# Layer scale with residual (x + gamma·y) on one core: row blocks of 4, 64 and 60 in place of 8, 60 and 60, and stores released by VectorE

## The chip, the core and the metric

The kernel runs on one core of a Trainium2 chip. The metric is the device time of one execution in microseconds (us); lower is better. Before the change it is 119.94 us, the median of three runs (119.84 to 120.05). The profiled execution spans 118.5 us from its first to its last instruction; the time counts a little more than that span.

## What is computed

```python
x: [1024, 16, 512] bf16      y: [1024, 16, 512] bf16      gamma: [512] bf16
out = x + gamma * y          # gamma is broadcast over the last dimension
```

Flattened, x, y and the output are 16,384 rows of 512 bf16 values, 1,024 bytes a row. Each of the 128 SBUF partitions holds 128 rows, so "60 rows" below always means 60 rows in each of 128 partitions: 60 KiB a partition and 7,680 KiB in all. The kernel reads 33.55 MB and writes 16.78 MB. The only arithmetic is one multiplication and one addition per element.

## The kernel before

All loads are issued by SyncE into one DMA queue, all stores by ScalarE into another. The 128 rows of a partition are cut into three blocks, and each block is one contiguous run of device memory per partition. VectorE works on four pieces: the pieces of 15 and 45 rows together are the second block.

```python
BLOCKS = [8, 60, 60]
PIECES = [8, 15, 45, 60]
SP = [                       # what SyncE loads, in this order: (tensor, first row, end row, slot in x_sb)
    ('y', 0, 8),
    ('y', 8, 68),
    ('x', 8, 68, 0),
    ('y', 68, 128),
    ('x', 68, 128, 15),      # its slots 15 to 75 overlap the slots 0 to 60 of x's rows 8 to 68
    ('x', 0, 8, 0),
]
ACT = [('g',), ('s', 8, 68), ('s', 68, 128), ('s', 0, 8)]     # gamma's load, then the three stores
EARLY = (2, 0)               # the first two loads stand ahead of the start barrier
RELEASE = ('x', 68, 128, 15)
DVE = [('m', 0), ('m', 1), ('m', 2), ('a', 2), ('a', 1), ('m', 3), ('a', 3), ('a', 0)]
```

y has its own 128 KiB a partition and is multiplied and added to in place; the stores read y_sb. x has a smaller buffer of 75 rows, so a later load of x waits until the sums that read its slots are done: x's rows 68 to 128 wait for the sum of piece 2 (`a, 2`), x's rows 0 to 8 for the sum of piece 1 (`a, 1`).

The stores have a gate of their own besides the sums that they need. TensorE waits for the load of x's rows 68 to 128, and then releases ScalarE (`s_go`) and VectorE (`s_rel`):

```python
    _take(s_load[RELEASE], 16, nc.tensor)      # TensorE waits for x's rows 68..128
    nc.tensor.sem_inc(s_go, 1)                 # ScalarE may issue the first store
    nc.tensor.sem_inc(s_rel, 1)                # VectorE may add piece 3
# ... (cut)
    for kind, *args in DVE:
        c = args[0]
        yt = y_sb[:, starts[c] : starts[c + 1], :]
        if kind == "m":
            need(y_loads, c)
            g = gamma_sb[:, None, :].to_broadcast([P, PIECES[c], D])
            nc.vector.tensor_tensor(out=yt, in0=yt, in1=g, op=MULT).then_inc(s_dve, 1)
            open_mults += 1
        else:
            need(x_loads, c)
            # ... (cut: waits for VectorE's own products)
            nc.vector.tensor_tensor(out=yt, in0=xt, in1=yt, op=ADD).then_inc(s_add, 1)
```

The gate keeps the stores out of the way of the large loads. gamma is spread over the 128 partitions by one small matmul with a row of ones, and copied from PSUM to SBUF.

Of the kernel before, what the change touches and what calls it, by code (L numbers as in the profile page):

```python
# [3 lines left out]

BLOCKS = [8, 60, 60]

PIECES = [8, 15, 45, 60]


SP = [
    ('y', 0, 8),
    ('y', 8, 68),
    ('x', 8, 68, 0),
    ('y', 68, 128),
    ('x', 68, 128, 15),
    ('x', 0, 8, 0),
]
ACT = [('g',), ('s', 8, 68), ('s', 68, 128), ('s', 0, 8)]  # L20

EARLY = (2, 0)

RELEASE = ('x', 68, 128, 15)

DVE = [('m', 0), ('m', 1), ('m', 2), ('a', 2), ('a', 1), ('m', 3), ('a', 3), ('a', 0)]
MULT, ADD = mybir.AluOpType.mult, mybir.AluOpType.add


def _take(sem, n, eng):  # L30


    return eng.wait_ge(sem, n).then_inc(sem, -n)  # L33


def kernel(
# [9 lines left out]
    nc = tc.nc  # L46
# [8 lines left out]
    rows = N // P  # L55
    n = len(PIECES)
    assert sum(PIECES) == rows
    starts = [sum(PIECES[:c]) for c in range(n + 1)]
    dt = xf.dtype
    edges = [sum(BLOCKS[:c]) for c in range(len(BLOCKS) + 1)]  # L60
    assert edges[-1] == rows

    def rows_of(t, a, b):

        c = max(c for c in range(len(BLOCKS)) if edges[c] <= a)
        assert b <= edges[c + 1]
# [6 lines left out]
    y_sb = nc.alloc_sbuf_tensor("y_sb", [P, rows, D], dt).ap()  # L73
    x_loads = [w for w in SP + ACT if w[0] == "x"]
    y_loads = [w for w in SP + ACT if w[0] == "y"]
    stores = [w for w in SP + ACT if w[0] == "s"]
    for loads in (x_loads, y_loads, stores):
# [5 lines left out]
    sem = nc.alloc_semaphore  # L83
    s_gamma, s_ones, s_ps, s_dve = sem("s_gamma"), sem("s_ones"), sem("s_ps"), sem("s_dve")
    s_load = {w: sem("s_" + "_".join(map(str, w[:2]))) for w in x_loads + y_loads}
    s_add, s_go, s_rel, s_end, s_out = sem("s_add"), sem("s_go"), sem("s_rel"), sem("s_end"), sem("s_out")
    added = [a for kind, *a in DVE if kind == "a"]
    order = {a[0]: k for k, a in enumerate(added)}

    def meets(a, b, c, d):  # L90
        return a < d and c < b
# [4 lines left out]
    def x_at(row):  # L96
        return next(w[3] + row - w[1] for w in x_loads if w[1] <= row < w[2])
# [12 lines left out]
    def ring(eng, what, n_early):  # L110

        known, went = 0, False
        for k, w in enumerate(what):
            kind = w[0]
            need = frees(w) if kind == "x" else pieces_of(w[1], w[2]) + list(w[3:]) if kind == "s" else []
            need = max((order[c] + 1 for c in need), default=0)
            if kind == "s" and not went:
                _take(s_go, 1, eng)
                went = True
            if need > known:  # L120
                eng.wait_ge(s_add, need)
                known = need
            if kind == "g":
                i = eng.dma_start(out=gamma_row, in_=gamma.unsqueeze(0)).then_inc(s_gamma, 16)
            elif kind == "x":
                to = x_sb[:, w[3] : w[3] + w[2] - w[1], :]
                i = eng.dma_start(out=to, in_=rows_of(xf, w[1], w[2])).then_inc(s_load[w], 16)
            elif kind == "y":
                r = slice(w[1], w[2])
                i = eng.dma_start(out=y_sb[:, r, :], in_=rows_of(yf, w[1], w[2])).then_inc(s_load[w], 16)  # L130
            else:
                r = slice(w[1], w[2])
                i = eng.dma_start(out=rows_of(of, w[1], w[2]), in_=y_sb[:, r, :]).then_inc(s_out, 16)
            if k < n_early:
                early.append(i.ins)

    ring(nc.sync, SP, EARLY[0])
    ring(nc.scalar, ACT, EARLY[1])

# [6 lines left out]
    nc.vector.tensor_copy(out=gamma_sb, in_=gamma_ps).then_inc(s_dve, 1)  # L146
    _take(s_dve, 1, nc.vector)

    _take(s_load[RELEASE], 16, nc.tensor)
    nc.tensor.sem_inc(s_go, 1)  # L150
    nc.tensor.sem_inc(s_rel, 1)

    landed, open_mults = set(), 0

    def need(loads, c):
        for w in loads:
            if w not in landed and meets(starts[c], starts[c + 1], w[1], w[2]):
                if w == RELEASE:
                    _take(s_rel, 1, nc.vector)
                else:  # L160
                    _take(s_load[w], 16, nc.vector)
                landed.add(w)

    for kind, *args in DVE:
        c = args[0]
        yt = y_sb[:, starts[c] : starts[c + 1], :]
        if kind == "m":
# [6 lines that stand above are left out]
            if open_mults:  # L174
                _take(s_dve, open_mults, nc.vector)
                open_mults = 0
            at = x_at(starts[c])
            xt = x_sb[:, at : at + PIECES[c], :]
            nc.vector.tensor_tensor(out=yt, in0=xt, in1=yt, op=ADD).then_inc(s_add, 1)  # L179
# [44 lines left out]
```

## Time and profile before

| What | Value |
|---|---|
| time, median of 3 runs | 119.94 us (119.84 to 120.05) |
| span of the profiled execution | 118.5 us |
| VectorE busy | 70.1 us (59% of the span) |
| TensorE busy | 0.6 us |
| bytes moved by DMA | 50.33 MB, mean 425 GB/s over the span |
| a product or sum of 60 rows (128x30720) on VectorE | 16.16 us |
| of 45 rows (128x23040) | 12.16 us |
| of 15 rows (128x7680) | 4.16 us |
| of 8 rows (128x4096) | 2.29 us |

An engine's row in the profile counts its arithmetic only. The instructions that issue a DMA take about 0.4 us of their queue's time and show when a transfer was asked for, not how long it ran; the transfer's own time is from its issue to its landing. A share of DMA over a stretch is the mean over the core's 16 DMA engines. In such a stretch a packet's bytes and time are booked at one point of the packet, so short stretches swing above and below 1; stretches of several packets are to be read.

### The profile page before, as it was taken

What the parts mean: (1) busy time and instruction counts of PE and PEld (TensorE: products, weight loads), DVE (VectorE), ACT (ScalarE), POOL (GpSimd) and SP (SyncE); (2) the same over time, 40 slices, a digit from 0 to 9 for tenths busy, and PEclk for the clock granted to TensorE, in tenths of its full rate; (3) what the DMA queues carried; (4) which work ended last, traced back from release to release, by engine and by line L of the source; (5) the groups of instructions that cost most, each with busy time, mean ns of one, the idle gap of its engine ahead of it and who ended that gap; (6) DMA issues with size and microseconds to landing.
All of it is one profiled execution on the core that took longest, in us unless ns stands there. A gap on an engine that the chain in (4) does not pass through costs nothing. (4 is left out here: it accounts for less than half of the span.)

```text
span 118.5 us, 81 instructions
## 1 busy us (share of the span) xinstructions
PE 0.6 (0%) x1; PEld 0.1 (0%) x1; DVE 70.1 (59%) x10; POOL 0.2 (0%) x4
## 2 busy tenths in 40 slices
PE   0001000000000000000000000000000000000000
PEld 0000000000000000000000000000000000000000
DVE  0005400299999399999499999469999950000000
POOL 0000000000000000000000000000000000000000
DMA  5999779779779779978977977897797797797787
GB/s 180 506 602 394 332 332 663 332 332 663 332 332 663 332 332 601 394 332 352 643 332 332 663 332 332 384 633 332 332 663 332 332 663 332 332 663 332 332 365 321
DMA packets 1298, 50.33 MB, mean 425 GB/s; under 512 B 145, under 2 KB 146, under 8 KB 146
## 3 DMA queue, kind: packets, MB, share of 16 engines
q1 hardware_dynamic: 864, 33.55, 65.8%
q10 hardware_dynamic: 434, 16.78, 32.7%
HBM read 33.56 MB, written 16.78 MB: 425 GB/s over the span
## 5 line engine op out<-in xcount | busy, mean ns | idle before, releaser
L170 DVE TENSOR_TENSOR y_sb<-y_sb,gamma_sb 128x4096 bf16<-128x4096 bf16 (+3 forms) x4 | 34.7, 8689 | 11.9 <-DVEq L33 11.9
L179 DVE TENSOR_TENSOR y_sb<-x_sb,y_sb 128x23040 bf16<-128x23040 bf16 (+3 forms) x4 | 34.6, 8688 | 4.5 <-DVEq L33 4.5
L146 DVE CAST gamma_sb<-gamma_ps 128x512 bf16<-128x512 f32 x1 | 0.7, 690 | 7.9 <-DVEq L33 7.9
L141 DVE MEMSET ones_row<- 1x128 bf16 x1 | 0.2, 165 | 2.0 <-PEq L49 2.0
L144 PE MATMUL gamma_ps<-gamma_row,ones_row 1*128 1x512 bf16 x1 | 0.6, 581 | 9.3 <-PEq L33 9.3
L144 PEld LDWEIGHTS gamma_ps<-gamma_row,ones_row 1*128 1x128 bf16 x1 | 0.1, 97 | 9.3 <-issue 9.3
L208 POOL MEMSET const-bfloat16-1.0<- 128x1 bf16 x1 | 0.1, 102 | 0.0
L208 POOL MEMSET const-uint8-127<- 128x1 uint8 x1 | 0.1, 102 | 0.0
L208 POOL MEMSET const-float32-0.0<- 128x1 f32 x1 | 0.1, 99 | 0.2 <-issue 0.2
L208 POOL MEMSET const-float32-1.0<- 128x1 f32 x1 | 0.1, 99 | 0.0
## 6 DMA issues: line engine op xcount, KB each, us to landing
y_sb<-in_y_dram SPq DMA_DIRECT2D x2, 7680.0 KB, 39.8
x_sb<-in_x_dram SPq DMA_DIRECT2D x2, 7680.0 KB, 31.5
out_dram<-y_sb ACTq DMA_DIRECT2D x2, 7680.0 KB, 21.0
y_sb<-in_y_dram SPq DMA_DIRECT2D x1, 1024.0 KB, 4.8
x_sb<-in_x_dram SPq DMA_DIRECT2D x1, 1024.0 KB, 22.3
out_dram<-y_sb ACTq DMA_DIRECT2D x1, 1024.0 KB, 22.1
gamma_row<-in_gamma_dram ACTq DMA_DIRECT2D x1, 1.0 KB
```

Source lines behind the costliest of these rows:

```text
L141: nc.vector.memset(ones_row, 1.0).then_inc(s_ones, 1)
L144: nc.tensor.matmul(gamma_ps, ones_row, gamma_row, start=True, stop=True).then_inc(s_ps, 1)
L146: nc.vector.tensor_copy(out=gamma_sb, in_=gamma_ps).then_inc(s_dve, 1)
L170: nc.vector.tensor_tensor(out=yt, in0=yt, in1=g, op=MULT).then_inc(s_dve, 1)
L179: nc.vector.tensor_tensor(out=yt, in0=xt, in1=yt, op=ADD).then_inc(s_add, 1)
L208: nc = _bacc.Bacc("TRN2", target_bir_lowering=False, num_devices=1)
```

## The change

The blocks become 4, 64 and 60 rows. y's first 4 rows come first, x's first 4 rows are the last load, and their output the last store. The middle block grows to 64 rows, which is 64 KiB contiguous per partition. x's buffer shrinks from 75 to 71 rows (slots 11 to 71 for x's last 60 rows). TensorE no longer takes part in the release: VectorE waits for its own product of y's last 60 rows, and then releases the stores, whether x's last 60 rows have landed or not. The purpose is to have the stores in their queue by the time the loads run out, with a smaller transfer left over at each end.

```diff
-BLOCKS = [8, 60, 60]
+BLOCKS = [4, 64, 60]
-PIECES = [8, 15, 45, 60]
+PIECES = [4, 11, 53, 60]
 SP = [
-    ('y', 0, 8),
-    ('y', 8, 68),
-    ('x', 8, 68, 0),
+    ('y', 0, 4),
+    ('y', 4, 68),
+    ('x', 4, 68, 0),
     ('y', 68, 128),
-    ('x', 68, 128, 15),
-    ('x', 0, 8, 0),
+    ('x', 68, 128, 11),
+    ('x', 0, 4, 0),
 ]
-ACT = [('g',), ('s', 8, 68), ('s', 68, 128), ('s', 0, 8)]
+ACT = [('g',), ('s', 4, 68), ('s', 68, 128), ('s', 0, 4)]
-RELEASE = ('x', 68, 128, 15)
-DVE = [('m', 0), ('m', 1), ('m', 2), ('a', 2), ('a', 1), ('m', 3), ('a', 3), ('a', 0)]
+DVE = [('m', 0), ('m', 1), ('m', 2), ('a', 2), ('a', 1), ('m', 3), ('go',), ('a', 3), ('a', 0)]
# ... (cut)
-    _take(s_load[RELEASE], 16, nc.tensor)
-    nc.tensor.sem_inc(s_go, 1)
-    nc.tensor.sem_inc(s_rel, 1)
# ... (cut: in need(), VectorE waits for every load's own semaphore, x's last 60 rows too)
     for kind, *args in DVE:
+        if kind == "go":
+            _take(s_dve, open_mults, nc.vector)
+            open_mults = 0
+            nc.vector.sem_inc(s_go, 1)
+            continue
         c = args[0]
```

More of the change, by code (lines that the diff above doesn't have):

```diff
@@ L85 @@
     s_load = {w: sem("s_" + "_".join(map(str, w[:2]))) for w in x_loads + y_loads}
-    s_add, s_go, s_rel, s_end, s_out = sem("s_add"), sem("s_go"), sem("s_rel"), sem("s_end"), sem("s_out")
+    s_add, s_go, s_end, s_out = sem("s_add"), sem("s_go"), sem("s_end"), sem("s_out")
     added = [a for kind, *a in DVE if kind == "a"]
@@ L157, in need @@
             if w not in landed and meets(starts[c], starts[c + 1], w[1], w[2]):
[L158 to L161, printed above, removed]
+                _take(s_load[w], 16, nc.vector)
                 landed.add(w)
     for kind, *args in DVE:
+        if kind == "go":
[3 more added lines that the diff above has]
+            continue
         c = args[0]
```

## The prediction

> **What bounds the kernel now.** I read the page's DMA rows first, because 50.33 MB against 70.1 us of VectorE work points there:
>
> ```profile
> DVE  0005400299999399999499999469999950000000
> ...
> DMA  5999779779779779978977977897797797797787
> ...
> q1 hardware_dynamic: 864, 33.55, 65.8%
> q10 hardware_dynamic: 434, 16.78, 32.7%
> HBM read 33.56 MB, written 16.78 MB: 425 GB/s over the span
> ```
>
> The two queues' packets fill 65.8 + 32.7 = 98.5% of the time of 16 DMA engines; q1 holds the loads, q10 the stores. The row's 7s and 9s are how long packets fall into slices, not idle engines: longer stretches (columns: stretch, length, PE, PEld, DVE, POOL, clock, DMA share, GB/s) give
>
> ```profile
> 42.50:58.30 15.80, 0.00 (x0) 0.00 (x0) 15.09 (x2) 0.00 (x0) 1.00 1.01 436
> 60.60:76.40 15.80, 0.00 (x0) 0.00 (x0) 14.96 (x1) 0.00 (x0) 1.00 1.00 436
> ...
> 98.20:113.90 15.70, 0.00 (x0) 0.00 (x0) 0.00 (x0) 0.00 (x0) 1.00 1.01 438
> ```
>
> Full at 436 GB/s while loading, and the same while storing with VectorE idle. Then the timelines of VectorE and of the two issuing queues, for the waits (start, length, instruction, idle time before):
>
> ```profile
> 23.10 16.23 DVE L170 TENSOR_TENSOR y_sb<-y_sb,gamma_sb 128x7680 bf16<-128x7680 bf16 x2 [9.79 <-DVEq L33]
> 41.36 16.23 DVE L179 TENSOR_TENSOR y_sb<-x_sb,y_sb 128x23040 bf16<-128x23040 bf16 x2 [2.04 <-DVEq L33]
> 59.40 16.16 DVE L170 TENSOR_TENSOR y_sb<-y_sb,gamma_sb 128x30720 bf16<-128x30720 bf16 x1 [1.81 <-DVEq L33]
> 78.05 18.36 DVE L179 TENSOR_TENSOR y_sb<-x_sb,y_sb 128x30720 bf16<-128x30720 bf16 x2 [2.49 <-DVEq L33]
> ```
>
> ```profile
> 53.55 4.39 SPq L127 DMA_DIRECT2D x_sb<-in_x_dram  x2
> ```
>
> ```profile
> 77.76 19.02 ACTq L133 DMA_DIRECT2D out_dram<-y_sb  x3
> ```
>
> Each group of VectorE starts when a load lands, idle before it; it waits for DMA, never DMA for it, as long as the next transfer is in its ring before the last runs out. The packet records of the trace let me look at the seams. The first packet begins at 1.03 us. x's last 60 rows end, engine by engine, between 76.67 and 76.97; x's 8 rows fill 76.67 to 79.43; the stores' first packets begin between 79.14 and 79.43, each within 0.01 to 0.02 us after the last load packet or its marker. The last packet ends at 118.11. So after the start no engine has a gap that I can find: **the bound is bytes over DMA rate**, and only 1.03 us ahead of the first packet and 0.4 us behind the last lie outside it.
>
> **What the Trainium skill says.** "DMA: Bandwidth & Descriptors", section "Where 436 GB/s comes from", gives 435.2 GB/s as the ceiling of the 16 SBUF ports. The trace agrees: 436 and 438 GB/s above. The kernel is at that ceiling, with nothing left to gain in rate. The same page, section "Queues, rings and completion order", says each DMA engine takes turns between its queues, a packet each. The trace agrees: gamma's 1 KB was issued at 1.91 us, its packet ran at 6.56, behind a 60 KiB packet, and its completion marker at 8.87, behind another; hence the matmul only at 9.34. The same page, section "Latency and other measured facts", warns that rows at large power-of-two pitches slow DMA copies: 512 KiB pitch 207 GB/s per direction against 214 padded, 2 MiB 164. The new 64 KiB block is a power of two, the old 60 KiB is not. No run here shows it yet. "VectorE: DVE Perf Modes", section "Side-by-side: where the cycles go for N=2048 bf16", gives two elements a cycle for a packed tensor_tensor; 30720/2/0.96 GHz = 16.0 us, and the trace has 16.16.
>
> **The change part by part.**
>
> 1. *DMA work.* A partition is one packet per transfer: 128 packets of 61440 bytes took 2.267 us each, those of 8192 bytes 0.309 us. The slope is (2.267 − 0.309)/53248 = 0.0368 us per 1000 bytes (27.2 bytes/ns, 16 engines 435 GB/s), the remainder 0.008 us per packet. With that I estimate 0.158 us for 4096 and 2.418 us for 65536 bytes. Each engine serves 8 partitions. Before: 24 small + 48 large = 24·0.309 + 48·2.267 = 116.23 us. After: 24·0.158 + 24·2.418 + 24·2.267 = 3.79 + 58.03 + 54.41 = 116.23 us. **Change 0.00 us**: bytes and packet count are the same.
>
> 2. *Where the loads land.* A 60-row load takes 59.40 − 41.36 = 18.04 us between two landings, 0.301 us a row. In front of y's rows 4–68 stand the same 68 rows in total, so piece 1's product still starts at 23.1. Rows up to and including x's middle block go from 128 to 132, so all landings from there on are 4·0.301 = 1.2 us later: the first sum at 42.6 (was 41.36), the product of y's last 60 rows at 60.6 (was 59.40), x's last 60 rows landed at 78.6 (the trace has 77.41 before).
>
> 3. *VectorE.* From 7680 and 30720 elements: (16.157 − 4.157)/23040 = 0.521 ns an element plus 0.157 us. So 53 rows (27136) cost 14.29 us, 11 rows (5632) 3.09, 4 rows (2048) 1.22. The sum of 53 rows: 42.6 + 14.3 = 56.9, when x's last load is issued (was 53.55). y's last rows leave their ring about 0.7 us ahead of their landing at 60.5, at 59.7. Taking 1.03 to 1.8 us from issue to packet (the first load's engines start between 1.03 and 1.83), the new packets are there by 58.7 at the latest: **1.0 us to spare, where it was 4.** x's 4 rows are issued at 56.9 + 3.1 = 60.0, far ahead. All this is hidden.
>
> 4. *The seam between loads and stores.* The product ends at 60.6 + 16.16 = 76.8. VectorE's own wait, ScalarE's release: about 0.2 us, so the first store is issued at 77.0 (was 77.76), and its packets are on the rings between 78.0 and 78.8. The loads of x's last 60 rows end between 76.67 + 1.2 = 77.9 and 78.2, and x's 4 rows would alone last until 79.4 as before (the same 256 rows). The stores come in time: **0.00 us**, no gap before and none after. With the old release they would have come at about 79 + 0.35 + 1.4 = 80.7, behind a gap of over 1 us; the new release pays for the smaller cover, it brings nothing net. The rest of x's 4 rows now takes turns with 64 KiB store packets: up to 8 turns (and the marker) of 2.4 us, landing between 80 and 98.
>
> 5. *The tail.* The sum of the last 60 rows starts at 78.8 and ends at 94.9; its store must be on the rings when the 64-row store runs out, at 79.4 + 8·2.418 = 98.8 at the latest, and is there by 96.8. The sum of 4 rows ends at worst near 100, and its store is needed near 98.8 + 18.1 = 116.9. Hidden. TensorE's two increments and wait lay beside the work: 0.
>
> Sum: 0.00 us on a path that stays DMA from 1.03 to 118.1.
>
> **Rivals.** (a) *The power-of-two pitch.* 192 of 384 row transfers (y, x and output of the 64-row block) change from 60 to 64 KiB pitch. If the loss were that of the quoted 512 KiB row, (214 − 207)/214 = 3%, on half the work of 116 us, it would cost 1.9 us. For it: all 16 engines now step through addresses equal in their low bits. Against: the pitch is eight times smaller than the one that still kept 97%. Time about 120.5 to 121.8. (b) *A late or early meeting at a seam.* If the new stores reach some engine ahead of the completion marker of x's last 60 rows, that marker waits one store packet, as gamma's did; the last large sum then ends near 97.5, its store comes near 99, and the rings run dry for up to 0.5 us. Or the 1.0 us to spare of step 3 is less than I think. Time 120.0 to 120.6. (c) *Turning between reads and writes costs something each time*, 8 turns on each engine; gamma's single turn shows no gap, and even 0.05 us a turn would be 0.4 us. (d) *A gain*: a shorter first and last packet. But the first packets of y were limited by latency (0.36 to 1.1 us against 0.309 later), so at most 0.15 us of packet comes sooner, with the bytes the same. Time 119.7.
>
> **Range and chances.** The base is 119.94 + 0.00; I lean 0.05 up, since three of four rivals cost and one gains. The low end is (d) with the scatter of the runs; the high end is (b) or (c), or a third of (a). A change over 2% is 2.4 us: faster by that would need more than the 435 GB/s of the ports, 1%; slower needs the full aliasing loss and more, 4%.
>
> **What would show it.** Step 1: DMA shares still sum to about 98.5%, 436 GB/s in the stretches inside the 64-row transfers. A lower rate there, and only there, is rival (a). Step 2: VectorE starts at 23.1, 42.6, 60.6, 78.8. Step 3: x's last load issued at 56.9, and no dip near 59. Step 4: first store issued near 77.0, no idle slice up to 82. Step 5: the second store issued near 95; at 97.6 rival (b) has happened. I am wrong if the 64 KiB packets take longer than 2.42 us or are cut into many small ones, or if rings run dry at a seam.

## The result and the profile after

The changed kernel takes 120.56 us, the median of 6 runs (120.30 to 120.82), against 119.94 us before (119.84 to 120.05). The ratio is 1.0051, with a 95% interval of 1.0036 to 1.0067: a small loss that is real, within the 2% band. The prediction's sum was 119.94 + 0.00 us, with 0.05 us added, so about 120.0; its rival (b) reached from 120.0 to 120.6. The time lies at the upper end of what the rivals allowed, and the central estimate missed nearly all of the loss.

The profile is of an execution of 120.82 us, the longest of the six, and that of the kernel before is of one of 119.86 us; so the loss read from the two is 0.3 us larger than between the medians. The page of the changed kernel first: the DMA row, the two queues, and the mean rate.

```profile
DMA  9888998889888987987998998798998899899874
...
q1 hardware_dynamic: 864, 33.55, 65.6%
q10 hardware_dynamic: 434, 16.78, 32.5%
HBM read 33.56 MB, written 16.78 MB: 421 GB/s over the span
```

The packet counts are those of before (864 and 434), and 65.6 + 32.5 = 98.1% of a span of 119.5 us is 117.2 us of packets per engine; before it was 98.5% of 118.5 us, 116.7 us. So the packets account for about half a microsecond of the full one by which the span grew. The rest is time in which engines stand idle. The last two digits, 7 and 4, say where. The end of the span, in stretches of one microsecond (stretch, length, PE, PEld, DVE, POOL, clock, DMA share, GB/s), for the changed kernel:

```profile
116.00:117.00 1.00, 0.00 (x0) 0.00 (x0) 0.00 (x0) 0.00 (x0) 1.00 0.39 160
117.00:118.00 1.00, 0.00 (x0) 0.00 (x0) 0.00 (x0) 0.00 (x0) 1.00 0.75 307
118.00:119.00 1.00, 0.00 (x0) 0.00 (x0) 0.00 (x0) 0.00 (x0) 1.00 0.14 57
```

and for the kernel before:

```profile
116.00:117.00 1.00, 0.00 (x0) 0.00 (x0) 0.00 (x0) 0.00 (x0) 1.00 1.00 426
117.00:118.00 1.00, 0.00 (x0) 0.00 (x0) 0.00 (x0) 0.00 (x0) 1.00 0.84 352
118.00:118.50 0.50, 0.00 (x0) 0.00 (x0) 0.00 (x0) 0.00 (x0) 1.00 0.01 0
```

Before, all engines stop together just after 118. After, most have stopped by 118, and a few work on for up to another microsecond (a share of 0.14, taken over all 16). A mean over 16 engines hides this: **the kernel ends with its slowest engine**.

VectorE's timeline and the two issuing queues, of the changed kernel:

```profile
23.06 17.29 DVE L166 TENSOR_TENSOR y_sb<-y_sb,gamma_sb 128x5632 bf16<-128x5632 bf16 x2 [9.48 <-DVEq L31]
42.52 17.29 DVE L175 TENSOR_TENSOR y_sb<-x_sb,y_sb 128x27136 bf16<-128x27136 bf16 x2 [2.16 <-DVEq L31]
60.55 16.16 DVE L166 TENSOR_TENSOR y_sb<-y_sb,gamma_sb 128x30720 bf16<-128x30720 bf16 x1 [0.74 <-DVEq L31]
79.41 17.30 DVE L175 TENSOR_TENSOR y_sb<-x_sb,y_sb 128x30720 bf16<-128x30720 bf16 x2 [2.70 <-DVEq L31]
```

```profile
56.84 3.33 SPq L125 DMA_DIRECT2D x_sb<-in_x_dram  x2
```

```profile
76.98 20.14 ACTq L131 DMA_DIRECT2D out_dram<-y_sb  x3
```

The predicted starts were 23.1, 42.6, 60.6 and 78.8 for VectorE, 56.9 and 77.0 for the queues. All agree within 0.1 us except the last sum, 0.6 us late. Something happened to the load of x's last 60 rows, between 60.5 and 79.4 us.

The trace holds the moment at which each of the 16 engines reports its part of a transfer as landed. From these records, the earliest, the mean and the latest engine (us):

```
                        before                 after
y's middle block    22.67  22.78  22.96    22.41  22.61  22.93
y's last 60 rows    58.97  59.09  59.27    59.89  60.11  60.42
x's last 60 rows    77.12  77.24  77.41    78.07  78.40  79.28
x's small block     79.61  79.72  79.90    79.34  79.68  80.77
last store         118.24 118.36 118.50   118.01 118.38 119.46
```

The mean engine finishes at 118.38 us, as before (118.36). The latest engine is 1.1 us behind the mean, where it was 0.14. It fell behind between y's last rows (0.3 us behind the mean) and x's last rows (0.9 us), and never caught up: at every later landing the latest is still 0.9 to 1.1 us behind the mean. Each engine has eight of the 128 packets of every transfer, and nothing in the trace shows another engine taking some over. In the packet records, the seam between y's last rows and x's last rows is at 59.6 to 60.2 us. There, one engine's first packet of x's last rows took 3.30 us, another's 2.77, where 2.27 is the rule, and a third stood empty for 0.36 us.

### The profile page after: what moved, and what is told of

It reads as the page before. It is cut to its first block, busy times and chain, and to the rows that moved or that the text cites. A ratio compares the mean times of both kernels' runs of the same rounds, so it can differ in the third digit from the quotient of the medians.

```text
span 119.5 us, 79 instructions
## 1 busy us (share of the span) xinstructions
PE 0.6 (0%) x1; PEld 0.1 (0%) x1; DVE 70.1 (59%) x10; POOL 0.2 (0%) x4
## 3 DMA queue, kind: packets, MB, share of 16 engines
q1 hardware_dynamic: 864, 33.55, 65.6%
q10 hardware_dynamic: 434, 16.78, 32.5%
## 5 line engine op out<-in xcount | busy, mean ns | idle before, releaser
L166 DVE TENSOR_TENSOR y_sb<-y_sb,gamma_sb 128x2048 bf16<-128x2048 bf16 (+3 forms) x4 | 34.7, 8690 | 10.5 <-DVEq L31 10.5
L175 DVE TENSOR_TENSOR y_sb<-x_sb,y_sb 128x27136 bf16<-128x27136 bf16 (+3 forms) x4 | 34.6, 8689 | 4.9 <-DVEq L31 4.9
```

## The experiments

A queue's ring, below, is what waits in it on each engine; it runs dry when the last packet issued so far ends. **Theory A**: x's last large load is issued too shortly before its ring runs dry. The change made that lead smaller, because the sum that frees the buffer grew from 45 to 53 rows, 2.1 us (it also started 1.2 us later, but the ring's end moved by 1.0 us too). Single engines then lose time at the seam and stay behind. **Theory B**: the 64 KiB rows are slower. **Theory C**: stores that come early disturb the loads. Below, "lead" is the time from the issue of x's last 60 rows to the end of y's last packet on the first engine that ends them, in that kernel's own trace (58.4 to 58.7 us with old blocks, 59.5 and 59.6 with new ones); "spread" is the time from the first engine's landing to the last one's.

### The change with a longer lead: x's last rows in slots 15 to 75

```diff
-PIECES = [4, 11, 53, 60]
+PIECES = [4, 15, 49, 60]
-    ('x', 68, 128, 11),
+    ('x', 68, 128, 15),
```

> The changed kernel with x's last 60 rows in slots 15 to 75 instead of 11 to 71 (pieces 4, 15, 49, 60): they wait for a sum of 49 rows instead of 53 and are issued near 55.8 us, 3.8 us ahead of the ring's end instead of 2.8. Theory A: the long first packets at that seam shrink or go, the last sum starts near 78.8 instead of 79.4, time 120.0 to 120.3 (the seam behind y's 4 rows stays, with some 0.2 to 0.35 us). Theory B: still 120.5, with 64 KiB rows as before.

120.00 us (119.79 to 120.25); ratio to before 1.0002, interval 0.9994 to 1.0010. **The loss is gone.** The issue of x's last rows and the last sum in this kernel's timelines:

```profile
55.70 4.40 SPq L125 DMA_DIRECT2D x_sb<-in_x_dram  x2
```

```profile
78.63 17.30 DVE L175 TENSOR_TENSOR y_sb<-x_sb,y_sb 128x30720 bf16<-128x30720 bf16 x2 [1.99 <-DVEq L31]
```

The load is issued 1.1 us sooner and the lead is 1.0 us longer. The last sum starts 0.8 us sooner, near the 78.8 us of the prediction's step 5. x's last rows land within 78.0 to 78.5 us, a spread of 0.50 instead of 1.21. The blocks, the 64 KiB rows and VectorE's release are those of the change. So none of these makes the loss by itself, and theory B falls.

### The kernel before with a shorter lead

Two kernels move x's last rows to lower slots. Old blocks, slot 7:

```diff
-PIECES = [8, 15, 45, 60]
+PIECES = [8, 7, 53, 60]
-    ('x', 68, 128, 15),
-    ('x', 0, 8, 0),
+    ('x', 68, 128, 7),
+    ('x', 0, 8, 67),
```

> Blocks of 8, 60 and 60 and TensorE's release as before; x's last 60 rows go to slots 7 to 67 (x's 8 rows to 67 to 75), so they wait for a sum of 53 rows instead of 45 and are issued near 55.7 us, 2.9 us ahead of the ring's end at 58.6, as in the changed kernel (2.8 us). Theory A: one or more engines have a first packet of x's last rows 0.3 to 1 us too long, the engines end 0.5 to 1.4 us apart, time 120.2 to 120.8. Theory B: no 64 KiB rows, so 119.9 and ends within 0.3 us.

120.69 us, ratio 1.0063 (1.0048 to 1.0077), as large a loss as the change's, with none of the change in it but the sum of 53 rows and so the lead. Slot 3 is the same with pieces of 3 and 57 rows, and x's small block in slots 63 to 71:

> As the one before, with x's last 60 rows in slots 3 to 63 (x's 8 rows in 63 to 71): they wait for a sum of 57 rows and are issued near 56.7 us, 1.9 us ahead of the ring's end. Theory A: worse than with slot 7, most engines with a long first packet or a short gap, time 120.5 to 121.5. Theory B: 119.9.

120.30 us, ratio 1.0030 (1.0018 to 1.0042): a loss, but smaller than with slot 7, not larger. I had expected the opposite.

In these two the place in the buffer changed as well. The next three leave every slot of the kernel before alone. x's last load waits for one sum more than its buffer needs, and the size of that sum sets the lead:

```diff
-PIECES = [8, 15, 45, 60]
+PIECES = [8, 7, 8, 45, 60]      # or 11 and 4, or 3 and 12, in place of 7 and 8
-DVE = [('m', 0), ('m', 1), ('m', 2), ('a', 2), ('a', 1), ('m', 3), ('a', 3), ('a', 0)]
+DVE = [('m', 0), ('m', 1), ('m', 2), ('m', 3), ('a', 3), ('a', 2), ('a', 1), ('m', 4), ('a', 4), ('a', 0)]
-            need = max((order[c] + 1 for c in need), default=0)
+            need = max((order[c] + 1 for c in need), default=0) + (w == RELEASE)
```

> Blocks, slots and release of the kernel before; the piece of 15 rows is cut into 7 and 8, and x's last load waits for one more sum (8 rows, 2.3 us), so it is issued near 55.8 us, 2.7 us ahead of the ring's end, with nothing moved in the buffer. Theory A (lateness of the load): as with slot 7, the landings of x's last rows spread over 0.6 to 1.2 us instead of 0.3, time 120.3 to 120.8. If it was the place in the buffer (slots 7 and 3) and not the lateness: spread 0.3 us, time 119.9 to 120.0.

> As the run with one sum later, but that sum has 4 rows instead of 8: x's last load is issued near 54.8 us, 3.8 us ahead of the ring's end (before: 5.0; with the 8-row sum: 2.8). Theory A with a limit between 2.9 and 3.8 us: as before, 119.9 to 120.1, landings of x's last rows spread over 0.3 us. Theory A without such a limit (the cost grows evenly as the lead shrinks): 120.3.

> The same with a sum of 12 rows: issued near 56.8 us, 1.7 us ahead. If the cost grows as the lead shrinks: 121 or more, worse than the 120.7 at 2.8 us. If the weak effect of the run with slot 3 (120.3 at 1.7 us) is the rule and a load issued some 3 us ahead is really worse than one issued 1.7 us ahead: 120.2 to 120.4.

| kernel | lead, us | time, us | ratio (95% interval) | spread of the engines at x's last rows, us | longest packet at the seam, us |
|---|---|---|---|---|---|
| before | 5.0 | 119.94 | 1 | 0.29 | 2.27 |
| old blocks, sum of 4 rows more | 3.8 | 120.01 | 1.0008 (1.0000 to 1.0017) | 0.38 | 2.27 |
| change with slot 15 | 3.8 | 120.00 | 1.0002 (0.9994 to 1.0010) | 0.50 | 2.28 |
| the change | 2.7 | 120.56 | 1.0051 (1.0036 to 1.0067) | 1.21 | 3.30 |
| old blocks, slot 7 | 2.8 | 120.69 | 1.0063 (1.0048 to 1.0077) | 0.91 | 2.75 |
| old blocks, sum of 8 rows more | 2.7 | 120.73 | 1.0067 (1.0054 to 1.0079) | 0.90 | 3.01 |
| old blocks, sum of 12 rows more | 1.7 | 120.41 | 1.0051 (1.0038 to 1.0063) | 0.76 | 2.74 |
| old blocks, slot 3 | 1.8 | 120.30 | 1.0030 (1.0018 to 1.0042) | 0.79 | 2.76 |

Each ratio is against executions of the kernel before that were taken beside it (median 119.88 to 119.96 us). Leads, spreads and packets are those of one execution each. The last column ties the loss to the seam: in the three kernels with a lead of 3.8 us or more, every packet there takes 2.27 or 2.28 us and no engine stands empty; in the five others the longest packet takes 2.74 to 3.30 us.

x's last load is issued, with the sum of 4 rows, with that of 12, and with that of 8, at

```profile
54.85 3.33 SPq L127 DMA_DIRECT2D x_sb<-in_x_dram  x2
```

```profile
56.79 1.20 SPq L127 DMA_DIRECT2D x_sb<-in_x_dram  x2
```

```profile
55.74 2.26 SPq L127 DMA_DIRECT2D x_sb<-in_x_dram  x2
```

The last of these kernels shows the reading best; its VectorE rows:

```profile
59.40 16.16 DVE L170 TENSOR_TENSOR y_sb<-y_sb,gamma_sb 128x30720 bf16<-128x30720 bf16 x1 [1.75 <-DVEq L33]
78.75 18.36 DVE L179 TENSOR_TENSOR y_sb<-x_sb,y_sb 128x30720 bf16<-128x30720 bf16 x2 [3.20 <-DVEq L33]
```

Up to 59.40 us its products and its first sum start within 0.01 us of those before. The difference is a load issued at 55.74 instead of 53.55, and the last sum starts 0.7 us later, at 78.75 instead of 78.05. Every kernel of the table with a lead of 3.8 us or more is within 0.1% of before, and every one with 2.8 us or less loses 0.3 to 0.7%. That a shorter lead costs, and that the change's lead was too short, is shown. How a load issued 2.8 us ahead can lengthen single packets is not: a cost that grows as the lead shrinks would make 1.7 us worse, and it was no worse, in two kernels. What happens inside the DMA engine stays open.

### The release

VectorE's release alone, on the old blocks and with the old lead:

```diff
-DVE = [('m', 0), ('m', 1), ('m', 2), ('a', 2), ('a', 1), ('m', 3), ('a', 3), ('a', 0)]
+DVE = [('m', 0), ('m', 1), ('m', 2), ('a', 2), ('a', 1), ('m', 3), ('go',), ('a', 3), ('a', 0)]
-    _take(s_load[RELEASE], 16, nc.tensor)      # and TensorE's two increments
```

> Blocks of 8, 60 and 60 as before, stores released by VectorE after the product of y's last 60 rows. Theory A (x's last large load is issued too shortly before its ring runs dry, so single DMA engines fall behind and stay behind): x's last load is issued at 53.6 us as before, 5.0 us ahead, so the time stays 119.9, the last sum starts within 0.2 us of 77.8 and the engines end within 0.3 us of each other. Theory C (the early release itself delays the loads): 120.4 or more, and a later last sum. Theory B (64 KiB rows): 119.9, there are none here.

120.98 us, ratio 1.0091 (1.0078 to 1.0104). Theory A's 119.9 missed; theory C holds here. The stores' issue, and two-microsecond stretches, in this kernel:

```profile
75.81 20.46 ACTq L131 DMA_DIRECT2D out_dram<-y_sb  x3
```

```profile
77.00:79.00 2.00, 0.00 (x0) 0.00 (x0) 1.47 (x1) 0.00 (x0) 1.00 0.98 332
```

At a DMA share of 0.98 the engines moved 332 GB/s, not 436: the packets were there, but long. In the packet records, x's small packets of 8 KiB take 0.309 us each up to 77.7 us, 1.9 us after the stores' issue. From then on many take 0.4 to 0.7 us, with gaps up to 0.6 between them. The first store packet shows at 79.62. VectorE's last sum ran beside these loads, but that is not the cause: in the kernel before it also ran beside x's last 8 rows, from 78.05 us on, and their packets stayed at 0.31 us. All engines lost: the mean landing of the last store went from 118.36 to 119.14 us.

Two more kernels vary the release on the new blocks with slot 15. An earlier one, after 53 of the 60 rows of the product:

```diff
-PIECES = [4, 15, 49, 60]
+PIECES = [4, 15, 49, 53, 7]
-... ('m', 3), ('go',), ('a', 3), ('a', 0)]
+... ('m', 3), ('go',), ('m', 4), ('a', 3), ('a', 4), ('a', 0)]
```

> Blocks of 4, 64 and 60 with slot 15; the product of y's last 60 rows is cut into 53 and 7 rows and VectorE releases the stores after the 53, near 74.9 us instead of 76.9. Theory C (stores that reach the engines while the last loads still run slow those loads): long load packets from about 76.8 us on, a later landing of x's last rows, time 120.8 or more. If the slow loads of the run with old blocks and new release had another cause: 120.0.

121.12 us, ratio 1.0105 (1.0090 to 1.0120), as theory C says. Its stores' issue, and its transfers of x, from issue to landing:

```profile
75.13 21.95 ACTq L131 DMA_DIRECT2D out_dram<-y_sb  x3
```

```profile
x_sb<-in_x_dram SPq DMA_DIRECT2D x1, 7680.0 KB, 23.3
...
x_sb<-in_x_dram SPq DMA_DIRECT2D x1, 512.0 KB, 30.5
```

In the kernel it was made from (slot 15), the same rows read:

```profile
76.91 19.56 ACTq L131 DMA_DIRECT2D out_dram<-y_sb  x3
```

```profile
x_sb<-in_x_dram SPq DMA_DIRECT2D x1, 7680.0 KB, 22.8
...
x_sb<-in_x_dram SPq DMA_DIRECT2D x1, 512.0 KB, 20.0
```

With stores issued at 75.13 us, x's last rows landed 0.6 us later and x's 4 rows more than ten. The large packets were slowed too: the last packet of x's 60 rows took 2.73 to 3.18 us on every engine, where 2.27 is the rule. Then the loads' last packets did take turns with store packets, as the prediction's step 4 had expected for the change itself. And TensorE's release, which waits for x's last rows:

```diff
-DVE = [..., ('m', 3), ('go',), ('a', 3), ('a', 0)]
+DVE = [..., ('m', 3), ('a', 3), ('a', 0)]
+    _take(s_load[RELEASE], 16, nc.tensor)      # and TensorE's two increments, as before
```

> Blocks of 4, 64 and 60 with x's last rows in slots 15 to 75, but stores released by TensorE once x's last 60 rows have landed (78.5 us). The prediction's step 4: stores issued near 78.8, their packets not before 80.2, while x's 4 rows end near 79.4: an empty stretch of about 1 us on all engines, time 120.7 to 121.2. If the release did not matter: 120.0.

120.51 us, ratio 1.0049 (1.0035 to 1.0062):

```profile
78.88 18.13 ACTq L133 DMA_DIRECT2D out_dram<-y_sb  x3
```

The loads' packets end between 78.9 and 79.4 us, the stores' begin at 79.74 to 79.89, and the engines are empty for 0.66 us on average between. The time stayed below the 120.7 to 121.2 us expected. So there is a window. Issued near 77 us the stores cost nothing; on these blocks 1.8 us earlier costs 1.0%, and 2.0 us later 0.5%. Counted back from the mean landing of the last load in the kernel without the loss (79.45 us with slot 15, 79.72 before), stores issued 2.5 and 2.0 us ahead cost nothing, 4.3 and 3.9 us ahead were too early, and 0.6 us ahead was too late.

### The first seam

The spread with slot 15 is 0.50 us, still above the 0.29 of before. It is already there when y's middle block lands (0.55 us), and the suspect was the seam between y's 4 rows and y's 64:

```diff
-    ('y', 0, 4),
-    ('y', 4, 68),
+    ('y', 4, 68),
+    ('y', 0, 4),
-DVE = [('m', 0), ('m', 1), ('m', 2), ('a', 2), ('a', 1), ('m', 3), ('go',), ('a', 3), ('a', 0)]
+DVE = [('m', 1), ('m', 2), ('a', 2), ('m', 0), ('a', 1), ('m', 3), ('go',), ('a', 3), ('a', 0)]
```

> Blocks of 4, 64 and 60 with slot 15, and y's 64-row block loaded first, y's 4 rows second, so the seam between a small first load and the large one at 2.6 us is gone. If that seam costs engines their step (0.16 to 0.36 us too long in the changed kernel), the landings of y's large block spread over 0.3 us instead of 0.5 and the time is 119.7 to 119.9. If the spread is made by the first packets themselves: 120.0, spread 0.5.

120.13 us, ratio 1.0018 (1.0011 to 1.0025). The spread fell to 0.37 us, but the mean engine was 0.3 us later from the start (both y transfers through at 22.86, against 22.52). A small first load starts the engines sooner and less evenly; in these two executions the sooner start was worth more, with the last engine's last store landed at 118.42 us with slot 15 and at 118.59 here. Neither expectation fits. The new order also moved the release to 77.64 us, so the seam at 2.6 us is not shown to cost anything by itself. No version here beats the kernel before.

## Why the prediction was right, and where it was not

- **The bound and step 1 held.** Packets and bytes are the same. In the changed kernel the 64 KiB packets took a mean of 2.418 us when stored and 2.429 when loaded, against the estimate of 2.418. Rival (a), the power-of-two pitch, did not happen: 120.00 us with slot 15 has all the 64 KiB rows. The warning in "DMA: Bandwidth & Descriptors", section "Latency and other measured facts", is about pitches from 512 KiB up; at 64 KiB no run here shows a loss.
- **Step 2 and the durations of step 3 held** to 0.1 us.
- **The verdict of step 3, "1.0 us to spare ... All this is hidden", failed.** Its term of 1.03 to 1.8 us from issue to packet was read from the first load, on empty engines. Under load, 2.7 us of lead was too little, and 3.8 was enough. ("Where it was 4" was not worked out with the same term: 58.6 − 53.55 − 1.8 gives 3.2.) The prediction named this as the second half of rival (b), and the loss of 0.6 us lies in the 0.1 to 0.7 us it gave there. But it entered the sum as zero, and one engine did stand empty at the seam, which the prediction had named as a sign of being wrong. That the total still fell among its ranges is owed to the allowance for the rival, not to the step. The sum itself had a fault as well: it added up the work of a mean engine, and here a delay of one engine was a delay of the end.
- **Step 4's "0.00 us, no gap" held, its detail did not.** The stores were issued at 76.98 as worked out, and with slot 15 the seam costs nothing. The turns of packets expected there did not come in the changed kernel: x's 4 rows landed by 80.8 us, not up to 98: the latest engine ran its eight packets of them in a row from 78.96 to 80.41, while other engines were storing from 78.97 on. With the old release I expected a gap of over 1 us, from 1.4 us between issue and packet. It was 0.66 us on average (with slot 15), since the stores' first packets came 0.9 to 1.0 us after their issue.
- **Rival (c) was not seen as stated**: where loads and stores did take turns, after the earlier release, the 16 engines stayed busy all the time from 80.1 to 88 us, with packets of the usual 2.418 and 0.159 us. But stores that wait behind loads lengthened the loads' packets in two kernels. With slot 15 the same release costs nothing, and alone on the old blocks it costs 0.9%, so it is the timing that escapes it. The prediction saw that the new blocks need the new release, but not that the new release needs the later product of the new blocks.
- **Step 5**: the last sum started at 79.41, not 78.8, for the reason of step 3, and its store was still early enough.
- **Rival (d)**: the small first load did bring its bytes sooner: with slot 15 the mean last landing is 118.10 us against 118.36, in one execution each, that of slot 15 being its shortest. The wider spread took most of it back (latest 118.42 against 118.50).

## What to carry to other kernels

When DMA is the bound, look at each engine's landing and not only at the mean share: here every engine had its own eight packets of each transfer, and the kernel ended with the engine that was delayed most. Before a change that lets a load wait for a longer sum, work out how far ahead of its ring's end it is issued; here 3.8 us was safe and 2.8 us was not. A release of stores had two sides here: too late left the engines empty, too early slowed the loads that were still running.

## What was not expected of the hardware

- A load issued 2.7 or 2.8 us ahead cost as much as or more than one issued 1.7 or 1.8 us ahead (1.0067 and 1.0063 against 1.0051 and 1.0030).
- Stores waiting in their queue changed the loads from 1.9 us after their issue on, long before a store packet shows in the records: 8 KiB packets of 0.309 us became up to 0.72 us, and with stores issued at 75.13 us 60 KiB packets of 2.27 us became 2.73 to 3.18.
- The first store packets came 0.9 to 1.0 us after their issue when the engines were empty.
